# A long-convolution kernel whose first stage loads 50 rows out of 64 in small strided pieces instead of whole blocks of 128 partitions

## The chip, the core and the metric

The kernel runs on one NeuronCore of a Trainium2 chip. The metric is device time in microseconds (us) for one launch, lower is better. Matmuls run on TensorE (PE in the profile; its weight loads are PEld), elementwise work on VectorE (DVE), ScalarE (ACT) and GpSimd (POOL). Transfers between HBM and the on-chip memory SBUF (128 partitions) are issued from three instruction queues: SyncE (SP), ACT and POOL. All of them are carried out by the same 16 DMA engines.

## The reference

The inputs are x and v of shape (4, 12800, 128), a table of positions of shape (12800, 64), and small weights. With S = 12800:

```python
h = (np.maximum(pos_emb @ w1, 0.0) @ w2) * np.exp(-0.01 * np.arange(S))[:, None]
y = irfft(rfft(x * v, n=2 * S, axis=1) * rfft(h, n=2 * S, axis=0), n=2 * S, axis=1)[:, :S]
z = x * y                                   # the long convolution, gated by x
gate = sigmoid(sum(conv_w[k] * shift(z, 4 - k) for k in range(5)))
out = (gate * (z @ w_val)) @ w_out
```

## The kernel before, in words

The long transform is cut in two: position n of the sequence is split into a slow index n1 (two halves j of N1 = 100) and a fast index n2 of N2 = 64. The work goes through three stages.

The **first stage** transforms x * v along n1, one n2 at a time (function spectra), and between these steps it computes the transform of the filter h out of the position table (generator filt). For each n2 the rows n1 and 99 - n1 are folded, so 50 rows (NF) are left for each pair of batches. The host lays them out as two halves of 64 rows (NH), 50 rows of data and 14 rows of zeros, one half on partitions 0 to 63 and the other on 64 to 127. In this input (xv) one n2 is 128 rows of 2048 numbers: x and v side by side.

The steps of one n2 are these. **fetch** (L311) loads one block of 128 x 2048 from xv to one of five buffers called ld, on SP. **product** (L317, DVE) multiplies the x half by the v half; for every second n2 the result goes to a tile u, for the others back to ld. **mirrored** (L325 and L326, DVE) takes two n2, q and 63 - q, and forms sum and difference, the tiles eo. **spectra** (L338, PE) multiplies them by the table fold, and ACT copies the result from PSUM to a tile st (L340), of which there are four. **store** (L345) writes st to a_u in HBM: 96 of its 100 rows from ACT's queue, the last 4 from POOL's. A pair of n2 thus costs two fetches, two stores, and 24 matmuls of 512 columns.

The order is written out by hand: at step n of 64 the program issues fetch(n + 7), product(n + 3), every second time mirrored, then spectra(n), as many steps of filt as a budget gives, and the store. The first 16 steps of filt (L257) read the position table, which comes in 16 loads of 128 x 400 numbers (function load_pos, L250, SP), each issued when a place in a sixth ld buffer is free. Later steps of filt are L275 to L277 (result in ag) and L286 to L300.

The **second stage** (50 steps p) loads a pair of spectra from a_u (L232) and its weights (L226) into the same six ld buffers, multiplies with the filter and transforms back along n2, and stores to c_y. From its step 34 on it also loads parts of c_y to ag for the third stage, 64 rows at first, then 16 and 80 (load_k, L207). The **third stage** transforms back along n1, gates, and does the short convolution and the two projections.

Completion of DMAs: the program hands out eight counters (DMAHW0 to DMAHW7 below) in turn to the DMAs of SP and ACT together. A DMA that gets a counter still in use waits on its queue until the DMA that had it before has landed. POOL's DMAs have eight of their own (DMASW).

Of the kernel before, what the change touches and what calls it, by code (L numbers as in the profile page):

```python
# [9 lines left out]
F32 = mybir.dt.float32  # L10
# [3 lines left out]
ALU = mybir.AluOpType  # L14
# [9 lines left out]
B, S, D, FO, KC = 4, 12800, 128, 64, 5  # L24
J, N1, N2 = 2, 100, 64
M = N1 * N2
KG = 8
NF, NH = N1 // 2, 64
R = 4
WARM = 2  # L30
NC1 = N1 // 2 + 1
# [3 lines left out]
def _tables():  # L35
# [7 lines left out]
    for r in (0, NH):  # L43
        fold[r:r + NF, 0, :N1] = np.cos(off) + np.sin(off)
        fold[r:r + NF, 1, :N1] = np.cos(off) - np.sin(off)
# [84 lines left out]
def tile_longconv_gate(  # L130
# [56 lines left out]
    def load():  # L187
        return ld.tile([128, 2048], F32, name="ld")
# [3 lines left out]
    ld_pool = tc.tile_pool(name="ld", bufs=6)  # L192
    ld = ld_pool.__enter__()
# [28 lines left out]
    def load_pair(p, n1=None):  # L222
        if p % PG == 0:
            n_p = min(PG, NP - p)
            wt = load().rearrange("p (k c e) -> p k c e", k=PG, c=4)[:, :, 0:3]
            nc.sync.dma_start(out=wt[:, 0:n_p], in_=t_w[:, p:p + n_p])  # L226
            weights.append(wt)
        a2 = load().rearrange("p (k j e) -> p k j e", k=2, j=J)
        if n1:
            load_a(a2, p, 0, n1)  # L230
        else:
            nc.sync.dma_start(  # L232
                out=a2.rearrange("p k j e -> p k (j e)"),
                in_=a_u[2 * p:2 * p + 2].rearrange("k s n e j b d -> (s n e) k (j b d)"))
        return a2, weights[-1][:, p % PG]

    with tc.tile_pool(name="p1", bufs=1) as p1, tc.tile_pool(name="ps1", bufs=1, space=PSUM) as ps1:
        g_sb = p1.tile([N1, J, FO, N2], F32, name="g_sb")

        GN, E, XB = 8, 4, 5  # L240
        held = [load() for _ in range(XB + 1)]
        PE1 = GN // 2 * N1
        pos_held = held.pop()[:, 0:2048 // PE1 * PE1].rearrange("p (i q a) -> p i q a", q=GN // 2, a=N1)
        parts, pos_ts = [(c0, j) for c0 in range(0, N2, GN) for j in range(J)], []

        def load_pos():
            if len(pos_ts) < len(parts):
                c0, j = parts[len(pos_ts)]
                t = pos_held[:, len(pos_ts) % (2048 // PE1)]
                nc.sync.dma_start(out=t.rearrange("p q a -> p (q a)"), in_=pos[j, c0 // GN])  # L250
                pos_ts.append(t)

        def filt():
            for i, (n0, j) in enumerate(parts):
                gp = ps1.tile([N1, GN, FO], F32, name="gp", bufs=2)
                for q in range(GN // 2):
                    nc.tensor.matmul(  # L257
                        out=gp[:, 2 * q:2 * q + 2].rearrange("a n e -> a (n e)"),
                        lhsT=pos_ts[i][:, q], rhs=w1bd, start=True, stop=True)
                nc.vector.scalar_tensor_tensor(  # L260
                    g_sb[:, j, :, n0:n0 + GN], gp.rearrange("a n e -> a e n"), 0.0,
                    win[:, j, n0:n0 + GN].unsqueeze(1).to_broadcast([N1, FO, GN]),
                    op0=ALU.max, op1=ALU.mult)
                load_pos()
                yield 1.5
# [41 lines left out]
        n_seq = [n for q in range(N2 // 2) for n in (q, N2 - 1 - q)]  # L307

        def fetch(i):
            t = held[i % XB]  # L310
            nc.sync.dma_start(out=t, in_=xv[n_seq[i]].rearrange("h q w j l b d -> (h q) (w j l b d)"))  # L311
            fetched[i] = t.rearrange("p (w e) -> p w e", w=2)

        def product(i):
            t = fetched.pop(i)
            u = p1.tile([128, J * 2 * XE], F32, name="u", bufs=1) if i % 2 == 0 else t[:, 0]
            nc.vector.tensor_tensor(u, t[:, 0], t[:, 1], op=ALU.mult)  # L317
            us[i] = u

        def mirrored(q):  # L320

            a, b = us.pop(2 * q), us.pop(2 * q + 1)
            eo = held_e[q % 2]
            for s, op in ((0, ALU.add), (1, ALU.subtract)):
                nc.vector.tensor_tensor(eo[:, s].rearrange("p j l e -> p (j l e)"), a, b, op=op)  # L325
                nc.vector.tensor_tensor(eo[:, s, :, 0], eo[:, s, :, 0], eo[:, s, :, 1], op=ALU.subtract)  # L326
            eos[q] = eo
# [22 lines left out]
        with tc.manual_schedule():  # L350
            held_e = [p1.tile([128, 2, J, 2, XE], F32, name=f"eo{i}") for i in range(2)]
            fetch(0)
            raws = [
# [5 lines left out]
            for i in range(1, XB):  # L359
                fetch(i)  # L360
                load_pos()
            product(0)
            product(1)
            mirrored(0)
            product(2)
            for i in (XB, XB + 1):
                fetch(i)
            for n in range(N2):
                q, s = divmod(n, 2)
                if n + XB + 2 < N2:  # L370
                    fetch(n + XB + 2)
                if n + 3 < N2:
                    product(n + 3)
                if s == 0 and q + 1 < N2 // 2:
                    mirrored(q + 1)
                st = spectra(q, s)
# [20 lines left out]
    with tc.tile_pool(name="p2", bufs=1) as p2, tc.tile_pool(name="psz", bufs=1, space=PSUM) as psz, \  # L397
# [62 lines left out]
        with tc.manual_schedule():  # L460
            for p in range(-1, NP + 1):
# [53 lines left out]
                if nxt:  # L515
                    spectrum(p + 1, 1)
                if old:
# [7 lines left out]
                    inverse(p - 1, 1, ((0, oa[:, 2]), (1, oa[:, 3, 0:PB]), (0, oc[:, 0]), (1, oc[:, 1])))  # L525

# [250 lines left out]
```

## Time and profile before

| what | us |
|---|---|
| median of three runs (lowest, highest) | 1134.86 (1127.76, 1135.0) |
| the profiled execution, its own time | 1130.9 |
| its span, first to last instruction | 1128.9 |
| start of the second stage's first matmul | 341.2 |

The profiled execution lies 4 us below the median, and 2 us of its time lie outside the span. Over the whole span PE is busy 92%, DVE 87%, POOL 62%, ACT 55%, and the DMA engines move 317 GB/s on average. These are means over three stages with different limits. The first stage is the first 341 us, so the views below are cut to it. In the lists of waits, "A <- B" says that A stood idle until B released it. SPq, ACTq and POOLq are the instruction queues that issue DMAs.

### The profile page before, as it was taken

The page shows a single profiled execution, that of the slowest core. Times are in us where ns is not written, and L with a number is a line of the kernel's source. Part 1 is how long each engine was busy: PE and PEld are TensorE (multiplying, and loading weights), DVE is VectorE, ACT ScalarE, POOL GpSimd, SP SyncE. Part 2 cuts the span into 40 slices and gives each one's busy share as a digit, 9 for nine tenths or more (in the row PEclk, how much of TensorE's full clock was granted, in tenths as well). Part 3 has the DMA queues.
Part 4 walks back from the last instruction along what each step waited for, and adds up shares of the span by engine and source line. Part 5 has one row for each costly group of instructions (what it writes and reads, how often), then busy time and mean ns, then how long its engine had stood idle before and what let it go on. Part 6 is the DMA issues. An engine that isn't in the chain of part 4 may idle for free.

```text
span 1128.9 us, 17155 instructions
## 1 busy us (share of the span) xinstructions
PE 1038.0 (92%) x6204; PEld 490.9 (43%) x6204; DVE 980.8 (87%) x1214; ACT 619.1 (55%) x1003; POOL 698.1 (62%) x405
## 2 busy tenths in 40 slices
PE   5789997977868999999999999979999999999996
PEld 2345654534423444444444444434444444444442
DVE  6677657888817999999999999739999999999997
ACT  1347665866642444444344444346767777767673
POOL 1111110100016888898898889638999899999981
PEclk9899999999986999999999999998999999999999
DMA  9999999999987788888988999566888888888842
GB/s 376 414 415 410 395 380 368 391 371 372 338 263 245 257 302 310 304 298 309 315 302 288 373 339 329 163 193 262 342 318 346 305 349 314 350 313 351 314 181 116
DMA packets 87771, 357.95 MB, mean 317 GB/s; under 512 B 9269, under 2 KB 18278, under 8 KB 65073
## 3 DMA queue, kind: packets, MB, share of 16 engines
q1 hardware_dynamic: 45768, 224.74, 55.0%
q10 hardware_dynamic: 39408, 129.18, 29.3%
q0 software_dynamic: 2512, 2.94, 0.9%
q8 instruction: 50, 0.82, 0.3%
q14 instruction: 33, 0.26, 0.1%
HBM read 225.76 MB, written 131.07 MB: 316 GB/s over the span
## 4 chain that ended last, share of the span: by engine, by line
PE 63%; DMA 22%; DVE 11%; ACT 3%; issue 1%; SPq 0%; ACTq 0%; DVEq 0%
PE c_ps L442 20%; DMA ld<-in_xv_dram 17%; PE sd L601 9%; PE z_ps L426 9%; PE o_ps L664 7%; PE v_ps L654 6%; PE tp L615 5%; PE fp L338 3%; DMA ld<-in_pos_dram 3%; PE c_ps L411 2%; DVE gt L643 2%; DVE eo L325 2%; DMA c_y<-c_sb 1%; DVE va L432 1%; DVE vb L432 1%
## 5 line engine op out<-in xcount | busy, mean ns | idle before, releaser
L628 POOL TENSOR_TENSOR ext<-yr,xr 128x400 f32<-128x400 f32 x120 | 304.4, 2538 | 38.1 <-DVE yr L626 32.7
L643 DVE SCALAR_TENSOR_TENSOR gt<-ext,cw,gt 128x1600 f32<-128x1600 f32 x128 | 242.7, 1896 | 2.4 <-ACT gt L640 2.4
L338 PE MATMUL fp<-eo,fold 64*128 64x512 f32 x768 | 194.8, 643 | 35.2 <-ACT st L340 19.0
L446 ACT COPY c_sb<-c_ps 128x1024 f32<-128x1024 f32 x100 | 101.3, 1013 | 207.3 <-PE c_ps L442 207.3
L345 POOL DMA_DIRECT2D a_u<-st x64 | 33.2, 519 | 290.4 <-ACT st L340 245.2
L340 ACT COPY st<-fp 128x1024 f32<-128x1024 f32 x128 | 126.7, 1016 | 117.9 <-PE fp L338 81.7
L442 PE MATMUL c_ps<-va,ld 64*128 64x512 f32 (+1 forms) x800 | 165.7, 554 | 0.0
L432 DVE TENSOR_TENSOR va<-z_ps,h_sb 128x2048 f32<-128x2048 f32 x50 | 114.5, 2290 | 30.4 <-PE z_ps L426 30.4
L426 PE MATMUL z_ps<-ld 64*64 64x512 f32 x800 | 123.0, 619 | 9.8 <-DMA ld<-a_u 8.7
L601 PE MATMUL sd<-ag,fold 100*64 100x512 f32 (+1 forms) x512 | 127.9, 617 | 2.9 <-DMA ag<-c_y 2.9
L509 POOL TENSOR_TENSOR va<-va,vb 128x1024 f32<-128x1024 f32 x49 | 116.0, 2367 | 15.9 <-DVE vb L432 15.9
L338 PEld LDWEIGHTS fp<-eo,fold 64*128 64x128 f32 x768 | 73.4, 199 | 115.4 <-issue 59.8
L442 PEld LDWEIGHTS c_ps<-va,ld 64*128 64x128 f32 x800 | 74.1, 189 | 112.2 <-issue 111.7
L664 PE MATMUL o_ps<-gd,wout 128*128 128x400 f32 x256 | 111.5, 517 | 10.7 <-DVE gd L659 9.8
L513 POOL TENSOR_TENSOR va<-va,vb 128x1024 f32<-128x1024 f32 x50 | 119.1, 2383 | 0.0
L432 DVE TENSOR_TENSOR vb<-z_ps,h_sb 128x2048 f32<-128x2048 f32 x50 | 114.0, 2281 | 0.0
L608 ACT COPY sd_sb<-sd 128x512 f32<-128x512 f32 x128 | 76.7, 599 | 57.6 <-PE sd L601 57.0
L654 PE MATMUL v_ps<-ext,wval 128*128 128x400 f32 x256 | 107.3, 501 | 0.0
L442 PE MATMUL c_ps<-vc,ld 64*128 64x512 f32 x400 | 94.2, 589 | 0.0
L615 PEld LDWEIGHTS tp<-ident,sd_sb 128*128 128x128 f32 x512 | 58.9, 142 | 79.2 <-PE sd L601 48.7
L510 POOL TENSOR_TENSOR vc<-vc,vd 128x768 f32<-128x768 f32 x49 | 89.2, 1820 | 1.9
L615 PE MATMUL tp<-ident,sd_sb 128*128 128x128 f32 x512 | 81.0, 283 | 4.7 <-ACT sd_sb L608 3.4
(86 smaller groups left out, 1484.9 us busy)
## 6 DMA issues: line engine op xcount, KB each, us to landing
ld<-in_xv_dram SPq DMA_DIRECT2D x64, 1024.0 KB
ag<-c_y SPq DMA_DIRECT2D x58, 1024.0 KB
c_y<-c_sb ACTq DMA_DIRECT2D x100, 512.0 KB
a_u<-st ACTq DMA_DIRECT2D x64, 768.0 KB
ld<-a_u SPq DMA_DIRECT2D x48, 1024.0 KB
xr<-in_xt_dram SPq DMA_DIRECT2D x31, 800.0 KB
out_dram<-o_sb ACTq DMA_DIRECT2D x31, 800.0 KB
ld<-in_tab_w_dram SPq DMA_DIRECT2D x12, 768.0 KB
```

Of the source, the lines that this page charges most:

```text
L338: nc.tensor.matmul(out=fp[:, h], lhsT=fold[r, w], rhs=eo[r, o, :, l], start=i == 0, stop=i == len(terms) - 1)
L340: nc.scalar.copy(out=st[:, o].rearrange("k j (h b) d -> k h j (b d)", h=2), in_=fp)
L426: nc.tensor.matmul(out=zs[c][half[h]], lhsT=wk[half[c], 0, half[h]], rhs=a2[half[c], h, j], start=True, stop=True)
L432: nc.vector.tensor_tensor(out, z.rearrange("p (b d) -> p b d", d=D).unsqueeze(1).to_broadcast([128, n, B, D]), h_sb.unsqueeze(2).to_broadc ...
L442: nc.tensor.matmul(out=c_ps[:, h, 0:n], lhsT=wk[half[h], 1 + c], rhs=vt[half[h]].rearrange("p b d -> p (b d)"), start=(i == 0), stop=(i == ...
L513: nc.gpsimd.tensor_tensor(va[:, 2:4], va[:, 2:4], vb[:, 2:4], op=ALU.add)
L601: nc.tensor.matmul(out=sd[c * N2:(c + 1) * N2], lhsT=inv[k, s // NG, c], rhs=ct[c][k, r * B * D:(r + 1) * B * D], start=True, stop=True)
L615: nc.tensor.transpose(out=tp[:, b], in_=t[:, b], identity=ident)
L628: nc.gpsimd.tensor_tensor(e[:, r0 + r], yr, xr, op=ALU.mult)
L643: nc.vector.scalar_tensor_tensor(gt, rows(t, k), cw[:, k:k + 1], gt, op0=ALU.mult, op1=ALU.add)
L654: nc.tensor.matmul(out=v_ps, lhsT=wval, rhs=rows(t)[:, r * ROW:(r + 1) * ROW], start=True, stop=True)
L664: nc.tensor.matmul(out=o_ps, lhsT=wout, rhs=gd, start=True, stop=True)
```

## The change

A pair of n2 now has one load step. The host puts the 50 rows of a half on 64 partitions in a new pattern (QROW): rows 0 to 47 on the partitions whose number modulo 8 is 0 to 5, six in each group of eight; rows 48 and 49 on partitions 6 and 38 of the half. The table fold is permuted in the same way, so PE's work is the same. The zeros are not loaded any more: two of the three buffers for a pair are set to zero once by DVE and POOL, and the loads leave those partitions alone. The third buffer gets its zeros with pair 0, which is loaded whole.

fetch(q) is now six DMAs on SP, each of 16 rows (partitions r, r + 8, ..., r + 120) of 4096 numbers, 16 KB a row and 256 KB a DMA, and one DMA on POOL of 4 rows (partitions 6, 38, 70, 102). For pair 0 it is eight DMAs on SP. There are three buffers of two blocks where five blocks were before. product writes both n2 of a pair to u. The position table is loaded in four DMAs of 128 x 1600 into the space of ag, which is written only after the table has been read. The six ld buffers become one tile, and the second stage takes its places from a list (spare), in the order in which they come free.

```diff
+KX = 6
+QROW = np.array([8 * (q // 6) + q % 6 if q < 48 else 6 + 32 * (q - 48) for q in range(NF)])
...
     for r in (0, NH):
-        fold[r:r + NF, 0, :N1] = np.cos(off) + np.sin(off)
-        fold[r:r + NF, 1, :N1] = np.cos(off) - np.sin(off)
+        fold[r + QROW, 0, :N1] = np.cos(off) + np.sin(off)
+        fold[r + QROW, 1, :N1] = np.cos(off) - np.sin(off)
...
     def load():
-        return ld.tile([128, 2048], F32, name="ld")
+        return ld[:, spare.pop(0)]
...
-    ld_pool = tc.tile_pool(name="ld", bufs=6)
-    ld = ld_pool.__enter__()
+    ld_pool = tc.tile_pool(name="ld", bufs=1)
+    ld = ld_pool.__enter__().tile([128, 6, 2048], F32, name="ld")
+    spare, used = [4, 5, 0, 1, 2, 3], {}
...
+            used["w", p // PG] = spare[0]
+        used["a", p] = spare[0]
...
-        GN, E, XB = 8, 4, 5
-        held = [load() for _ in range(XB + 1)]
+        GN, E, XB = 8, 4, 3
         PE1 = GN // 2 * N1
-        pos_held = held.pop()[:, 0:2048 // PE1 * PE1].rearrange("p (i q a) -> p i q a", q=GN // 2, a=N1)
-        parts, pos_ts = [(c0, j) for c0 in range(0, N2, GN) for j in range(J)], []
-
-        def load_pos():
-            if len(pos_ts) < len(parts):
-                c0, j = parts[len(pos_ts)]
-                t = pos_held[:, len(pos_ts) % (2048 // PE1)]
-                nc.sync.dma_start(out=t.rearrange("p q a -> p (q a)"), in_=pos[j, c0 // GN])
-                pos_ts.append(t)
+        parts = [(c0, j) for c0 in range(0, N2, GN) for j in range(J)]
+
+        pos_ts = ag.rearrange("p k j e -> p (k j e)")[:, 0:len(parts) * PE1].rearrange(
+            "p (i q a) -> p i q a", q=GN // 2, a=N1)
+
+        def load_pos(i):
+            nc.sync.dma_start(out=pos_ts[:, 4 * i:4 * i + 4].rearrange("p i q a -> p (i q a)"), in_=pos[i])
...
-                        lhsT=pos_ts[i][:, q], rhs=w1bd, start=True, stop=True)
+                        lhsT=pos_ts[:, i, q], rhs=w1bd, start=True, stop=True)
...
-                load_pos()
...
-        n_seq = [n for q in range(N2 // 2) for n in (q, N2 - 1 - q)]
-
-        def fetch(i):
-            t = held[i % XB]
-            nc.sync.dma_start(out=t, in_=xv[n_seq[i]].rearrange("h q w j l b d -> (h q) (w j l b d)"))
-            fetched[i] = t.rearrange("p (w e) -> p w e", w=2)
-
-        def product(i):
-            t = fetched.pop(i)
-            u = p1.tile([128, J * 2 * XE], F32, name="u", bufs=1) if i % 2 == 0 else t[:, 0]
-            nc.vector.tensor_tensor(u, t[:, 0], t[:, 1], op=ALU.mult)
-            us[i] = u
+        def fetch(q):
+            t = ld[:, 2 * (q % XB):2 * (q % XB) + 2].rearrange("p e n -> p (e n)")
+            for r in range(KX if q else 8):
+                nc.sync.dma_start(out=t[r:128:8], in_=xv[q, r])
+            if q:
+                nc.gpsimd.dma_start(out=t[KX:128:32], in_=xv[q, KX, 0:16:4])
+            fetched[q] = t.rearrange("p (e w n) -> p e w n", e=2, w=2)
+
+        def product(q):
+            t = fetched.pop(q)
+            us[q] = p1.tile([128, 2, J * 2 * XE], F32, name="u", bufs=1)
+            for e in range(2):
+                nc.vector.tensor_tensor(us[q][:, e], t[:, e, 0], t[:, e, 1], op=ALU.mult)
...
-            a, b = us.pop(2 * q), us.pop(2 * q + 1)
+            u = us.pop(q)
             eo = held_e[q % 2]
             for s, op in ((0, ALU.add), (1, ALU.subtract)):
-                nc.vector.tensor_tensor(eo[:, s].rearrange("p j l e -> p (j l e)"), a, b, op=op)
+                nc.vector.tensor_tensor(eo[:, s].rearrange("p j l e -> p (j l e)"), u[:, 0], u[:, 1], op=op)
...
+            for q in range(1, XB):
+                (nc.vector, nc.gpsimd)[q - 1].memset(ld[:, 2 * q:2 * q + 2], 0.0)
             fetch(0)
+            load_pos(0)
...
-            for i in range(1, XB):
-                fetch(i)
-                load_pos()
             product(0)
+            mirrored(0)
+            for q in range(1, XB):
+                fetch(q)
+                load_pos(q)
+            load_pos(XB)
             product(1)
-            mirrored(0)
-            product(2)
-            for i in (XB, XB + 1):
-                fetch(i)
+            fetch(XB)
+            fetch(XB + 1)
             for n in range(N2):
                 q, s = divmod(n, 2)
-                if n + XB + 2 < N2:
-                    fetch(n + XB + 2)
-                if n + 3 < N2:
-                    product(n + 3)
                 if s == 0 and q + 1 < N2 // 2:
                     mirrored(q + 1)
+                if s == 1 and q + 2 < N2 // 2:
+                    product(q + 2)
+                    if q + 2 + XB < N2 // 2:
+                        fetch(q + 2 + XB)
                 st = spectra(q, s)
...
+                    spare.append(used.pop(("a", p + 1)))
...
+                    if p % PG == 0:
+                        spare.append(used.pop(("w", p // PG - 1)))
...
-    xv = np.concatenate([xv, np.zeros_like(xv[:, :, :NH - NF])], 2)
+    xz = np.zeros(xv.shape[:2] + (NH,) + xv.shape[3:], xv.dtype)
+    xz[:, :, QROW] = xv
+    xz = np.stack([xz[:N2 // 2], xz[:N2 // 2 - 1:-1]], 1).reshape(N2 // 2, 2, 16, 8, -1)
+    xv = np.transpose(xz, (0, 3, 2, 1, 4)).reshape(N2 // 2, 8, 16, -1)
     pos = np.asarray(inputs["pos_emb"]).reshape(J, N1, N2 // KG, KG // 2, 2, FO)
-    pos = np.transpose(pos, (0, 2, 4, 5, 3, 1)).reshape(J, N2 // KG, 2 * FO, KG // 2 * N1)
+    pos = np.transpose(pos, (2, 0, 4, 5, 3, 1)).reshape(4, 4, 2 * FO, KG // 2 * N1)
+    pos = np.transpose(pos, (0, 2, 1, 3)).reshape(4, 2 * FO, 2 * KG * N1)
```

On SP, which carries the loads, these are the first issues before and after (ld<-in_xv_dram is a load of x and v, in_pos_dram the position table):

```order
L311 DMA ld<-in_xv_dram 128x2048 x2
L250 DMA ld<-in_pos_dram 128x400
L311 DMA ld<-in_xv_dram 128x2048
L250 DMA ld<-in_pos_dram 128x400
L311 DMA ld<-in_xv_dram 128x2048
L250 DMA ld<-in_pos_dram 128x400
```

```order
L312 DMA ld<-in_xv_dram 16x4096 x8
L254 DMA ag<-in_pos_dram 128x1600
L312 DMA ld<-in_xv_dram 16x4096 x6
L254 DMA ag<-in_pos_dram 128x1600
L312 DMA ld<-in_xv_dram 16x4096 x6
L254 DMA ag<-in_pos_dram 128x1600 x2
L312 DMA ld<-in_xv_dram 16x4096 x174
```

The position table moved to the front, four issues where 16 were spread over the first 16 steps, and 64 loads of x and v became 194. In the middle of the stage, again on SP, with what each issue waits for (DVE is the product that frees the buffer), before and after:

```order
L311 DMA ld<-in_xv_dram 128x2048 [waits DMAHW4_49,DVE_49]
L311 DMA ld<-in_xv_dram 128x2048 [waits DMAHW6_49,DVE_49]
L311 DMA ld<-in_xv_dram 128x2048 [waits DMAHW0_49,DVE_49]
L311 DMA ld<-in_xv_dram 128x2048 [waits DMAHW2_49,DVE_49]
L311 DMA ld<-in_xv_dram 128x2048 [waits DMAHW4_49,DVE_49]
```

```order
L312 DMA ld<-in_xv_dram 16x4096 [waits DMAHW6_49,DVE_49]
L312 DMA ld<-in_xv_dram 16x4096 [waits DMAHW7_49]
L312 DMA ld<-in_xv_dram 16x4096 [waits DMAHW0_49]
L312 DMA ld<-in_xv_dram 16x4096 [waits DMAHW1_49]
L312 DMA ld<-in_xv_dram 16x4096 [waits DMAHW2_49]
L312 DMA ld<-in_xv_dram 16x4096 [waits DMAHW4_49]
L312 DMA ld<-in_xv_dram 16x4096 [waits DMAHW6_49,DVE_49]
```

Before, a load used the counter of the load four earlier (4, 6, 0, 2, then 4 again), now that of the load six earlier, which is the same piece of the pair before. The six pieces of one pair and its two stores take up all eight counters. On POOL, the first stores of the last 4 rows (a_u<-st) and what stands ahead of them, before and after:

```order
L182 DMA win<-in_tab_win_dram 100x128
L180 DMA w1bd<-in_w_dram 64x64 x2
L345 DMA a_u<-st 4x2048 x2
L388 DMA fwd<-in_tab_fwd_dram 100x300
L345 DMA a_u<-st 4x2048
```

```order
L185 DMA win<-in_tab_win_dram 100x128
L356 MEMSET ld 128x4096
L183 DMA w1bd<-in_w_dram 64x64 x2
L314 DMA ld<-in_xv_dram 4x4096 x4
L348 DMA a_u<-st 4x2048
L314 DMA ld<-in_xv_dram 4x4096
L348 DMA a_u<-st 4x2048
L394 DMA fwd<-in_tab_fwd_dram 100x300
```

POOL's queue now holds a load that waits for a product on DVE ahead of every second store. PE's and ACT's instructions are the same and in the same order in all three stages.

## The prediction

> **What bounds the kernel now.** I read the profile in this order: the rows in 40 slices, the chain that ended last (cut to the first 345 us), the DMA queues, then the waits. Of the slices:
>
> ```profile
> DMA  9999999999987788888988999566888888888842
> GB/s 376 414 415 410 395 380 368 391 371 372 338 263 245 257 302 310 304 298 309 315 302 288 373 339 329 163 193 262 342 318 346 305 349 314 350 313 351 314 181 116
> ```
>
> One slice is 28.2 us. In the first eleven the DMA engines are busy nine tenths or more and move 338 to 415 GB/s. The edit is in these slices. Their chain:
>
> ```profile
> by line: DMA ld<-in_xv_dram 54.4%; PE fp L338 9.7%; DMA ld<-in_pos_dram 8.7%; DVE eo L325 5.5%; ACT st L340 2.9%; DVE ld L317 2.8%; DVE eo L326 2.6%; DVE u L317 2.3%; DMA a_u<-st 1.9%; DVE fk L289 1.9%; issue 1.3%; PE gp L257 0.9%; DMA ld<-
> ...
> 1.19 7.95 DMA ld<-in_xv_dram
> ...
> 15.78 13.44 DMA ld<-in_pos_dram
> ...
> 29.70 16.68 DMA ld<-in_pos_dram
> ...
> 341.17 2.11 PE z_ps L426 x8
> ```
>
> 63% of the chain is loads. The first two loads of 1 MB needed 7.95 us together; a position load of 0.2 MB that takes 16.68 stands in line behind others. The second stage begins at 341.17. So the first stage ends when its bytes are through, and each edit is worth what it does to the time of the 16 DMA engines. How full these are, and what each queue gets out of them, in the 232 us between start and end (first the windows, with PE, PEld, DVE, ACT, POOL, clock, DMA share and GB/s; then the queues, q1 from SP, q10 from ACT, q0 from POOL):
>
> ```profile
> 64.00:296.00 232.00, 204.99 (x1550) 114.76 (x1552) 176.44 (x276) 156.42 (x244) 26.17 (x50) 0.97 0.99 385
> ```
>
> ```profile
> q1 hardware_dynamic: 6965, 49.60, 56.0%
> q10 hardware_dynamic: 5357, 37.63, 40.5%
> q0 software_dynamic: 1617, 1.75, 2.6%
> ```
>
> A share of 0.99 leaves no slack. A queue's MB over its share of the window is its rate had it all 16 engines: SP's loads 49.60 / (0.560 x 232 us) = 382 GB/s, ACT's stores 37.63 / (0.405 x 232) = 400, POOL's pieces 1.75 / (0.026 x 232) = 290.
>
> **The change, part by part.** The sizes:
>
> ```profile
> ld<-in_xv_dram SPq DMA_DIRECT2D x64, 1024.0 KB
> a_u<-st ACTq DMA_DIRECT2D x64, 768.0 KB
> ```
>
> ```profile
> ld<-in_pos_dram SPq DMA_DIRECT2D x16, 200.0 KB
> a_u<-st POOLq DMA_DIRECT2D x64, 32.0 KB, 6.7
> ```
>
> *Removed.* A pair of n2 loads 2 x 1024 KB = 2.097 MB, which is 2.097 / 0.382 = 5.49 us of all engines. After the change it is 6 x 256 KB = 1.573 MB on SP and 64 KB = 0.066 MB on POOL, the latter 0.066 / 0.290 = 0.23 us. Were SP's rate to stay, a pair would cost 1.573 / 0.382 + 0.23 = 4.35 us, 1.14 us less, and the 31 pairs behind pair 0 35 us less. This is the good end.
>
> *The rate of the new pieces.* The trace has no DMA of 16 rows eight partitions apart. It has loads of fewer than 128 rows: those of L207, 64 neighbouring rows in the second stage. Four are issued there, the first and the last here:
>
> ```profile
> 605.39 0.52 SPq L207 DMA_DIRECT2D ag<-c_y  x1
> ...
> 635.70 0.47 SPq L207 DMA_DIRECT2D ag<-c_y  x1
> ```
>
> The stretches in which these four were carried, and their q1:
>
> ```profile
> 606.70:609.90 3.20, 3.20 (x26) 1.46 (x26) 3.20 (x5) 1.14 (x2) 2.61 (x3) 1.00 1.00 214
> 616.00:619.80 3.80, 3.80 (x38) 1.31 (x34) 3.80 (x6) 2.07 (x4) 3.49 (x3) 1.00 1.02 302
> 632.10:635.80 3.70, 3.70 (x38) 1.54 (x38) 3.70 (x3) 2.15 (x4) 3.65 (x2) 1.00 1.01 276
> 641.80:648.40 6.60, 6.60 (x52) 2.88 (x48) 6.60 (x7) 2.79 (x5) 5.73 (x4) 1.00 1.04 353
> ```
>
> ```profile
> q1 hardware_dynamic: 120, 0.68, 99.7%
> ...
> q1 hardware_dynamic: 167, 0.82, 69.3%
> ...
> q1 hardware_dynamic: 132, 0.67, 72.1%
> ...
> q1 hardware_dynamic: 295, 1.34, 58.7%
> ```
>
> The engines count as fully busy and yet move 214 to 353 GB/s. In each, 0.524 MB are the 64-row load; the rest of q1 are loads over 128 partitions, which I take out at 382 GB/s. What is left: 0.524 / (3.19 - 0.41) = 188 GB/s, 0.524 / (2.63 - 0.77) = 282, 0.524 / (2.67 - 0.38) = 229, 0.524 / (3.87 - 2.14) = 301. These loads filled 87%, 49%, 62% and 26% of the engines' time: the more of it they fill, the slower they are, as if they blocked each other but not the stores. Six loads of 16 neighbouring rows (L207 too) come lower still, in the 7.0 us from 725.4 on:
>
> ```profile
> q1 hardware_dynamic: 190, 0.77, 64.7%
> ```
>
> 0.77 / (0.647 x 7.0) = 170 GB/s. So rows few in number and close together are slow. The new pieces are as few as these but spread as wide as a full load, so the 64-row load lies between the two ends, and I take it. In the changed stage stores keep about 40% of the engines as in q10's row, loads the rest, which lies between the 49% and 62% cases: the middle of 282 and 229, 256 GB/s. A pair then costs 1.573 / 0.256 + 0.23 = 6.37 us, 0.88 more than now, 27.3 us over 31 pairs. The other ends: 282 gives +10, 229 gives +50, 188 (no stores beside) +96.
>
> [...]
>
> *Pair 0* is loaded in eight pieces, 2.097 MB, and no store runs beside them: at 188 GB/s 11.2 us in place of 5.5, +5.7 us before PE can start.
>
> *Positions.* PE no longer stands still for the 13.4 and 16.7 us of the two position loads in the chain. But the engines carry these 3.28 MB as before, at full share, so the stall goes to the next load of x and v: 0. If DMA were not full it would be worth up to those 30 us.
>
> *SP's issues.* Two per pair become six:
>
> ```profile
> 40.37 0.33 SPq L311 DMA_DIRECT2D ld<-in_xv_dram  x1
> ```
>
> ```profile
> SPq L311 <- DMA ld<-in_xv_dram: 162.1, 40, 8.1
> ```
>
> 6 x 0.33 = 2.0 us; a pair takes nearly 10 (5.49 of loads and, at 400 GB/s, 2 x 0.786 / 0.400 = 3.9 of stores): hidden. The second row shows SP standing until an earlier load lands, its counter being taken. Four loads (4.2 MB) could be under way, now six pieces (1.6 MB). A load lands 7.95 - 5.49 = 2.5 us later than its bytes alone need; with 0.33 us for the issue a piece's place is empty for 2.8 us, while the five others keep the engines for 5 x 0.262 / 0.256 = 5.1 us: hidden. If they land together, the cover is gone and a pair costs 2.8 us more.
>
> *Waits on POOL and ACT.* POOL's piece waits for DVE's product, and every second 4-row store stands behind it. Its store takes 6.7 us to land, and the tile st is wanted again only four n2, some 20 us, later: 0. ACT's store now waits for the store two n2 back, about 10 us old, and ACT's copies stand behind it; a store's 0.79 MB take 2.0 us, 3.9 when loads take turns with them, and 2.5 to land: 0, with PE waiting for st if not.
>
> ```profile
> 1.01 0.27 DVE L176 MEMSET w2bd<- 128x256 f32 x1
> ```
>
> ```profile
> L509 POOL TENSOR_TENSOR va<-va,vb 128x1024 f32<-128x1024 f32 x49 | 116.0, 2367 | 15.9 <-DVE vb L432 15.9
> ```
>
> *The two memsets* of 4096 a partition: DVE 16 x 0.27 = 4.3 us, POOL between that and 4 x 2.37 = 9.5. Pair 0 needs longer, and pair 2, which waits for POOL, stands behind pair 1: 0. Products are the same 64. The second stage's new list of places lets loads start no later: 0.
>
> *Sum*: 27.3 + 5.7 = +33 us; span 1128.9 + 33 = 1161.9, and with the 2 us outside it **1164 us**, 2.6% above the median of the runs.
>
> **The rivals.**
>
> *The loads keep their rate* (faster). For it: the rows reach over all 128 partitions, and stores take turns with them at nearly 1 to 1, so two loads seldom need to meet. Against: the stretch at 49%, with stores beside, still gave 282. The end is -35 us; but PE sets a part of the stage:
>
> ```profile
> 113.00:170.00 57.00, 56.06 (x626) 33.88 (x624) 36.25 (x55) 37.42 (x40) 6.33 (x13) 1.00 1.00 388
> ```
>
> In these 57 us, some six pairs, PE has no gap, so 6 x 1.14 = 7 us can't be had: 1131 - 28 = **1103**. It decides from about 330 GB/s on: 1.573 / 0.330 + 0.23 = 5.00, -0.49 x 31 = -15, +5.7 for pair 0.
>
> *It cancels*: at 301 GB/s a pair costs 5.23 + 0.23 = 5.46, the same as now, and pair 0 leaves +5: **1136**. For it: the stretch with most else beside. Against: loads there filled only 26%.
>
> *Bytes are not removed at all*: the rows of zeros would have to be free now. Against it the 1024 KB of each load. No chance of its own.
>
> *Slower still*: six pieces land together and the queue runs empty, 2.8 us a pair on top (33 + 87 = +120), or the rate is 188 all through (+96 + 5.7 = +102): **1233 to 1251**. Against: stores fill such gaps.
>
> **How the numbers follow.** My forecast, 229 to 282 GB/s, with 1147 to 1187 us: 0.50. Slower still: 0.12. Cancels: 0.18. Rate kept: 0.20. The range leaves out the best of the faster cases and the worst of the slower: 1104 to 1195. About 1% is what measurement can tell from no change. Slower by more than 1% means over 1146, which from 1131 takes a rate under 282, so it has the forecast and the still slower case: 0.62. Within 1%: 0.18. Faster: 0.20.
>
> **What would show it.** In the changed profile the page's read bytes fall by some 13 MB; the first twelve slices still show nine tenths of DMA but under 360 GB/s; SP's queue moves its MB at 230 to 280 GB/s of full share where it had 382; the second stage's first matmul comes near 374 us instead of 341; position loads are gone from the chain; the stages behind are unchanged. A first stage under 330 us, or a rate of q1 over 330 GB/s, would prove me wrong; a DMA share well under 0.95 there would mean that a queue runs dry, not that rows are slow.

## The result and the profile after

| | before | after |
|---|---|---|
| median (runs of the comparison) | 1132.88 us (4) | 1164.89 us (4; 1163.16 to 1167.13) |
| ratio after / before, 95% interval | | 1.0315 [1.0282, 1.0348] |
| span of the profiled execution | 1128.9 us | 1161.4 us |
| start of the second stage's first matmul | 341.17 us | 374.86 us |

The change is 3.1% slower, 32 us, and the whole loss lies in the first stage. From the second stage's first matmul to the end, before needs 1128.9 - 341.2 = 787.7 us and after 1161.4 - 374.9 = 786.5. That matmul in after's timeline (start, length in us, in brackets the idle time ahead and what ended it):

```profile
374.86 3.80 PE L432 MATMUL z_ps<-ld 64*64 64x512 f32 x16 [7.39 <-DMA ld<-a_u]
```

The slices and the bytes on the page of after (a slice is now 29.0 us):

```profile
DMA  9999999999998688888888998685888888888842
GB/s 208 241 328 320 313 305 309 327 310 326 318 344 273 255 291 304 302 290 307 293 302 303 338 375 306 228 212 210 337 332 318 351 301 347 323 340 328 328 186 113
...
HBM read 211.53 MB, written 131.07 MB: 295 GB/s over the span
```

The same last row on the page of before:

```profile
HBM read 225.76 MB, written 131.07 MB: 316 GB/s over the span
```

14.2 MB less are read, just what the diff takes out (31 pairs x 0.459 MB). The first twelve digits of the DMA row are still 9: the engines count as full all the time, and carry less. The windows of after say how much less (columns as in the prediction):

```profile
0.00:28.00 28.00, 9.40 (x38) 4.72 (x40) 10.01 (x9) 3.31 (x3) 7.19 (x11) 1.00 0.95 204
28.00:56.00 28.00, 6.03 (x20) 3.21 (x18) 13.91 (x15) 1.93 (x2) 2.80 (x5) 0.61 1.02 234
64.00:296.00 232.00, 201.00 (x1520) 109.59 (x1518) 163.13 (x240) 135.80 (x196) 40.26 (x73) 0.95 0.98 319
```

and the start of before in the same windows:

```profile
0.00:28.00 28.00, 15.44 (x68) 7.99 (x68) 18.83 (x22) 5.33 (x5) 3.71 (x10) 1.00 0.95 375
28.00:56.00 28.00, 20.52 (x100) 10.87 (x102) 18.54 (x22) 9.83 (x10) 5.36 (x10) 0.88 1.02 414
```

The DMA share (last but one) is the same in both kernels. The rate is about half over the first 56 us, and 319 against 385 GB/s after that. So there are two losses, and the windows size both:

- *Steady.* A pair was 2.097 MB of loads and 1.573 MB of stores, at 385 GB/s 9.53 us. Now it is 1.639 + 1.573 = 3.212 MB, at 319 GB/s 10.07 us: +0.54 us, over 31 pairs +17 us.
- *Start.* In 56 us the engines moved 28 x (0.204 + 0.234) = 12.3 MB. At the steady 319 GB/s it would have been 17.9, so 5.6 MB are late: 5.6 / 0.319 = 17.5 us. In before the same 56 us moved 22.1 MB, about what its steady rate of 385 GB/s gives (21.6).

Together some 34 us. The queues of after in the steady window tell which transfers are slow:

```profile
q1 hardware_dynamic: 4205, 34.37, 48.7%
q10 hardware_dynamic: 5096, 35.84, 43.2%
q0 software_dynamic: 2441, 3.53, 5.8%
```

Per full share: SP's loads 34.37 / (0.487 x 232) = 304 GB/s (382 before), ACT's stores 35.84 / (0.432 x 232) = 358 (400), POOL's pieces 3.53 / (0.058 x 232) = 262 (290). The stores were not touched by the change and are slower all the same. The chain of after, cut to 380 us:

```profile
by line: DMA a_u<-st 46.2%; DMA ld<-in_xv_dram 24.9%; PE fp L341 10.2%; DMA ld<-in_tab_w_dram 4.2%; ACT st L343 4.0%; PE ap L277 2.9%; issue 1.4%; SPq L312 1.1%; DVE u L321 0.7%; DMA ld<-a_u 0.6%; DVE va L438 0.6%; DVE vb L438 0.6%; ACTq L3
...
47.34 10.72 DMA ld<-in_xv_dram
...
68.53 11.03 DMA a_u<-st
```

Loads up to 58 us, then mostly stores (46.2%), with the position loads gone. DMA holds three quarters of it, where the lines of before's chain that the prediction shows add up to two thirds. Why a store ends the chain is in the waits of ACT (total us, times, longest):

```profile
ACT st L343 <- DMA ld<-in_xv_dram: 43.1, 5, 26.6
ACT st L343 <- DMA a_u<-st: 41.9, 16, 4.5
```

ACT's copies stand behind its stores, and its stores behind their counters. The one wait of 26.6 us is for the first store, whose counter belongs to a load of pair 3, issued at 36.9 us and landed at 51.3 (the expectation of experiment 3 calls it a load of pair 4). Its group in the timeline, after and then before:

```profile
L348 ACTq DMA_DIRECT2D a_u<-st x64: 310/310/354, 51.3 to 366.3; - x64
```

```profile
L345 ACTq DMA_DIRECT2D a_u<-st x64: 310/311/358, 19.0 to 331.3; - x64
```

The first store is 32 us late, the last one 35. It is tempting to call this wait the cause. The third experiment shows that it is not the main one.

### The profile page after: what moved, and what is told of

It reads as the page before. It is cut to its first block, busy times and chain, and to the rows that moved or that the text cites. A ratio compares the mean times of both kernels' runs of the same rounds, so it can differ in the third digit from the quotient of the medians.

```text
span 1161.4 us, 17425 instructions
## 1 busy us (share of the span) xinstructions
PE 1042.3 (90%) x6204; PEld 488.6 (42%) x6204; DVE 983.4 (85%) x1215; ACT 616.5 (53%) x1003; POOL 721.1 (62%) x437
## 4 chain that ended last, share of the span: by engine, by line
PE 64%; DMA 26%; DVE 5%; ACT 4%; issue 1%; SPq 0%; ACTq 0%; DVEq 0%
PE c_ps L448 20%; DMA a_u<-st 15%; PE sd L610 10%; PE z_ps L432 9%; DMA ld<-in_xv_dram 8%; PE o_ps L673 7%; PE v_ps L663 6%; PE tp L624 5%; PE fp L341 3%; PE c_ps L417 2%; DMA ld<-in_tab_w_dram 1%; DVE gt L652 1%; ACT st L343 1%; DVE va L438 1%; PE ap L277 1%
## 5 line engine op out<-in xcount | busy, mean ns | idle before, releaser
L341 PE MATMUL fp<-eo,fold 64*128 64x512 f32 x768 | 200.9, 660 | 76.9 <-ACT st L343 58.3
L328 DVE TENSOR_TENSOR eo<-u 128x1024 f32<-128x1024 f32 x64 | 78.0, 1219 | 33.2 <-PE fp L341 32.9
L321 DVE TENSOR_TENSOR u<-ld 128x1024 f32<-128x1024 f32 x64 | 75.4, 1219 | 19.4 <-DMA ld<-in_xv_dram 18.8
```

The lines of the kernel that those rows point to most:

```text
L341: nc.tensor.matmul(out=fp[:, h], lhsT=fold[r, w], rhs=eo[r, o, :, l], start=i == 0, stop=i == len(terms) - 1)
```

## The experiments

The theories, as the expectations name them. **A**: what is slow is where a piece's 16 rows lie; the author's guess is that rows 32 partitions apart get in each other's way, and a piece with rows 8 apart is full of them. **B**: a DMA of few rows is slow wherever they lie. **C**: it is the regrouping (pairs in one buffer of 2 blocks, positions first, three buffers) and not the pieces. **D**: it is the start, where the first stores wait for the counters of pairs 3 and 4. **E**: it is the row's length, 16 KB in place of 8. **G**: it is the shared counters: eight DMAs a pair use all of them, so that stores and loads wait for each other.

All intervals are 95% and of the ratio to before, measured beside it. The code cuts show the lines that matter; those of experiments 10 to 12 are against experiment 6, the others against the change.

**1. Rows 7 apart** (A against B). The six pieces of a pair lie on partitions 8 + r, 15 + r, ... instead of r, r + 8, ...; the fold table is permuted to match.

```diff
-                nc.sync.dma_start(out=t[r:128:8], in_=xv[q, r])
+                nc.sync.dma_start(out=t[8 + r:8 + r + 106:7] if q else t[r:128:8], in_=xv[q, r])
...
-                nc.gpsimd.dma_start(out=t[KX:128:32], in_=xv[q, KX, 0:16:4])
+                nc.gpsimd.dma_start(out=t[21:106:28], in_=xv[q, KX, 0:16:4])
```

> The six pieces of a pair take rows 7 partitions apart (from partition 8 + r) in place of 8, so that of the 16 rows of a piece hardly two lie 32 partitions apart; number, size and order of the DMAs, the memsets and pair 0 stay. The 4 rows of POOL move to partitions 21, 49, 77, 105. Theory A (rows 32 partitions apart block each other): a 16 KB row alone falls from 1.23 us towards 0.62 to 0.8, SP's rate between 64 and 296 us rises from 304 to over 360 GB/s, ACT's stores from 358 to over 385, the first store leaves before 40 us in place of 51, time 1105 to 1135. Theory B (small pieces, few rows, few DMAs under way are slow as such): nothing moves, 1165 within 4.

Measured: 1157.21 us (1149.95 to 1158.63), ratio 1.0204 [1.0151, 1.0256]. Between the two. The queues of this kernel in the steady window:

```profile
q10 hardware_dynamic: 5341, 37.51, 46.4%
q1 hardware_dynamic: 4208, 34.46, 43.7%
```

SP's loads went from 304 to 34.46 / (0.437 x 232) = 340 GB/s with nothing changed but the place of the rows: so the place matters. But the stores, at 37.51 / (0.464 x 232) = 348, did not rise with them, and most of the loss stayed. Neither theory had this.

**2. One whole load per pair** (C). The new program as it is, but each pair comes in one DMA of 128 rows of 16 KB, zeros and all.

```diff
-            for r in range(KX if q else 8):
-                nc.sync.dma_start(out=t[r:128:8], in_=xv[q, r])
-            if q:
-                nc.gpsimd.dma_start(out=t[KX:128:32], in_=xv[q, KX, 0:16:4])
+            nc.sync.dma_start(out=t, in_=xv[q])
```

> Each pair is loaded whole, zeros too, by one DMA of 128 rows of 16 KB; pairs, positions in ag, order and memsets stay, POOL's piece goes. Theories A and B: SP's rate is back at 380 GB/s, stores at 400, time 1120 to 1140. Rival C (the loss comes from loading in pairs, from the prologue's order or from the list of places): it stays over 1155 although 14 MB more are moved at the old rate.

Measured: 1126.92 us, ratio 0.9963 [0.9941, 0.9986]. Its windows:

```profile
0.00:28.00 28.00, 14.49 (x68) 7.61 (x68) 21.66 (x22) 7.10 (x7) 7.17 (x11) 1.00 0.95 380
64.00:296.00 232.00, 203.26 (x1528) 110.69 (x1526) 172.88 (x274) 150.80 (x239) 24.86 (x47) 0.96 0.98 388
```

The rates of before are back, 380 and 388 GB/s, with rows of 16 KB. C falls: all that the change does beside the pieces is worth 4 us in its favour. The pieces cost the 32 us and these 4, though they load 22% less.

**3. Pairs 3 and 4 fetched later** (D). The two fetches stand behind the first two stores, so that these get free counters.

```diff
-            fetch(XB)
-            fetch(XB + 1)
...
+                if n < 2:
+                    fetch(XB + n)
```

> The fetches of pairs 3 and 4 move from the prologue to behind the first and second store in program order, so that the first stores on ACT don't get counters that those loads hold. Theory D (the start is lost because ACT's first store waits 26 us for a load of pair 4, so that loads run without stores beside them): the first store leaves at 25 to 35 us in place of 51, GB/s in the first 56 us rise from 219 to over 270, time 1140 to 1155. Theory A alone: the same bytes at the same mutual blocking, 1160 to 1168.

Measured: 1160.19 us (1159.97 to 1163.7), ratio 1.0259 [1.0222, 1.0295]. The group of stores in its timeline:

```profile
L348 ACTq DMA_DIRECT2D a_u<-st x64: 310/311/342, 38.5 to 364.8; - x64
```

The first store came 13 us sooner (38.5 against 51.3), the last only 1.5, and the intervals of the two ratios overlap. The first 56 us moved 216 and 258 GB/s in the two windows, 237 on average, short of the 270 that D asked for, and the steady window 315. D falls as the main cause.

**4. Rows of 8 KB** (E). Each row of a piece is read from two places of 8 KB.

```diff
+            t2 = t.rearrange("p (e n) -> p e n", e=2)
...
-                nc.sync.dma_start(out=t[r:128:8], in_=xv[q, r])
+                nc.sync.dma_start(out=t2[r:128:8], in_=xv[q, r].rearrange("e i n -> i e n"))
```

> Each 16 KB row is read from two places of HBM, 8 KB each, so that it should travel as two packets of 8 KB; all else stays. Theory E (rows of 16 KB take two of three turns at an engine and starve the stores, whose packets are 8 KB): ACT's stores go from 358 GB/s to over 380, time 1150 to 1160. Theory A: a row costs twice 0.62 us alone, stores as before, 1165 within 5.

Measured: 1154.43 us (1149.97 to 1161.11), ratio 1.0205 [1.0152, 1.0259]. Its steady window and the queues in it:

```profile
64.00:296.00 232.00, 208.37 (x1570) 113.43 (x1569) 178.37 (x266) 144.76 (x215) 44.07 (x78) 0.96 1.01 335
```

```profile
q1 hardware_dynamic: 6567, 35.88, 49.7%
q10 hardware_dynamic: 5386, 37.83, 44.5%
```

335 GB/s where the change has 319; the loads at 35.88 / (0.497 x 232) = 311, the stores at 366. A part of the loss, some 10 us, goes away with shorter rows. The time lies in E's range, but the stores stay under the 380 that E asked for, the loads themselves are hardly faster, and the second experiment has 16 KB rows at full speed. E is a side effect at most.

**5. A ruler.** Ahead of the kernel's own work, test loads of 16 rows of 16 KB on SP, first one at a time, then streams of six without waits between.

```diff
+            for start, step, n in ((0, 8, 16), (11, 7, 16), (8, 7, 16), (0, 1, 16), (0, 4, 8)):
+                for j in range(4):
+                    piece(1, j, start, step, n)
+                pause()
+            for starts, step in (((0,) * 6, 8), (tuple(range(6)), 8), ((11,) * 6, 7), (tuple(range(8, 14)), 7)):
+                for j, start in enumerate(starts):
+                    piece(j, j, start, step)
+                pause()
```

piece(i, j, start, step, n) loads n rows into buffer i, to the partitions start, start + step and so on; pause() issues nine tiny loads that set the groups apart.

> The changed kernel with test loads ahead of its first stage (SP only, nothing else on the DMA engines, results overwritten later). One at a time, four each, 16 KB rows: 16 rows 8 apart; 16 rows 7 apart from 11; 16 rows 7 apart from 8; 16 neighbours; 8 rows 4 apart. Then six without a wait between them: 8 apart from 0; 8 apart from 0 to 5; 7 apart from 11; 7 apart from 8 to 13. [...] Theory B (16 rows are slow as such): 1.0 to 1.23 for each, whatever the step. Its time as a whole says nothing.

Windows within the four streams of its one run: 8 apart, all on the same partitions; 8 apart from 0, 1, ... 5; 7 apart on the same partitions; 7 apart from 8, 9, ... 13:

```profile
137.00:143.00 6.00, 0.00 (x0) 0.00 (x0) 0.00 (x0) 0.00 (x0) 0.00 (x0) 1.00 0.94 190
161.00:166.00 5.00, 0.00 (x0) 0.00 (x0) 0.00 (x0) 0.00 (x0) 0.00 (x0) 1.00 0.99 210
185.00:189.00 4.00, 0.00 (x0) 0.00 (x0) 0.00 (x0) 0.00 (x0) 0.00 (x0) 1.00 0.78 262
207.00:211.00 4.00, 0.00 (x0) 0.00 (x0) 1.60 (x1) 0.00 (x0) 1.41 (x1) 1.00 0.85 262
```

A row's mean time on its engine is 16 engines x 16.4 KB x share / rate, that is 0.262 MB x share / rate (with 200 GB/s as 0.200 MB/us): 8 apart 1.30 and 1.24 us, 7 apart 0.78 and 0.85. So pieces 8 apart, by themselves and with nothing else running, move 190 to 210 GB/s, about what the change's start shows (204 and 234). Single loads, one at a time, hardly told the spacings apart: four of them were issued within 10.9 us with rows 8 apart, within 9.2 and 10.0 us with rows 7 apart, and within 12.6 us as 16 neighbours.

**6. Pieces of 32 rows, 4 apart.** Three pieces of 512 KB instead of six of 256 KB; 48 rows on the partitions with numbers 0 to 2 modulo 4, the last two of a half on 3 and 35. Same bytes as the change, but three loads and two stores a pair on the eight shared counters where the change has six and two. A in its first form has to call them as slow, since they too hold partitions 32 apart.

```diff
-KX = 6
+KX = 3
...
-QROW = np.array([8 * (q // 6) + q % 6 if q < 48 else 6 + 32 * (q - 48) for q in range(NF)])
+QROW = np.array([4 * (q // 3) + q % 3 if q < 48 else 3 + 32 * (q - 48) for q in range(NF)])
...
-                nc.sync.dma_start(out=t[r:128:8], in_=xv[q, r])
+                nc.sync.dma_start(out=t[r:128:4], in_=xv[q, r])
...
-                nc.gpsimd.dma_start(out=t[KX:128:32], in_=xv[q, KX, 0:16:4])
+                nc.gpsimd.dma_start(out=t[KX:128:32], in_=xv[q, KX, 0:32:8])
```

> [...] Theory A: 1160 to 1168. Theory G (the counters: only two stores and six small loads under way): 1140 to 1152, and ACT's waits for a store before fall under 20 us.

Measured: **1107.07 us** (1104.13 to 1110.92), ratio **0.9794 [0.9758, 0.9829]**. Faster than both kernels, and missed by both expectations. Its windows and, in the steady one, its queues:

```profile
0.00:28.00 28.00, 10.39 (x48) 5.47 (x48) 18.49 (x19) 3.35 (x4) 8.30 (x13) 1.00 0.94 321
28.00:56.00 28.00, 26.03 (x126) 13.80 (x128) 22.74 (x26) 11.62 (x12) 8.37 (x15) 0.88 1.01 397
64.00:296.00 232.00, 214.68 (x1612) 117.09 (x1612) 188.17 (x296) 164.81 (x260) 42.22 (x76) 0.99 0.98 360
```

```profile
q10 hardware_dynamic: 5822, 40.83, 47.0%
q1 hardware_dynamic: 4212, 38.95, 45.9%
```

Loads at 38.95 / (0.459 x 232) = 366 GB/s, stores at 374, the start at 321 and 397. The change's idea, fewer bytes, does pay when the pieces have this shape.

**7. The start alone.** The change, with pairs 0 to 4 loaded whole (from an input of their own), the others in pieces.

```diff
+            if q < 5:
+                nc.sync.dma_start(out=t, in_=xw[q])
+            for r in range(KX if q >= 5 else 0):
...
-            if q:
+            if q >= 5:
```

> Pairs 0 to 4 are loaded whole by one DMA of 128 rows, pairs 5 to 31 in pieces as before. It splits the loss between the start, where loads run alone, and the rest. If the start costs what the traces say (eighth store 29 us later than before the change, of which some 20 us remain at the end), 1140 to 1148; if the prediction's split were right (5.7 us for the start, 27 us for the pieces further on), 1156 to 1162.

Measured: 1145.26 us, ratio 1.0123 [1.0088, 1.0157]. 20 us of the loss are the start, as its expectation said for that case; the windows above gave 17.5.

**8. Without POOL's 4-row loads.** Rows 48 and 49 are left out of pairs 1 to 31.

```diff
-            if q:
-                nc.gpsimd.dma_start(out=t[KX:128:32], in_=xv[q, KX, 0:16:4])
```

> POOL's load of 4 rows is left out of pairs 1 to 31, so rows 48 and 49 of each half are missing in what is computed. If these loads cost only their share of the engines (0.23 to 0.3 us a pair), 1155 to 1159; if POOL's wait for the product holds up stores, under 1150; if they are hidden, 1164 within 3.

Measured: 1151.78 us, ratio 1.0196 [1.0157, 1.0234], between the cases of its expectation: 13 us less than the change (give or take some 6, an estimate from the two intervals), where their bytes at POOL's rate are 31 x 0.23 = 7. The start of this kernel:

```profile
0.00:28.00 28.00, 9.27 (x40) 4.72 (x40) 13.98 (x13) 3.31 (x3) 6.06 (x9) 1.00 0.96 232
28.00:56.00 28.00, 8.80 (x36) 4.25 (x36) 12.91 (x15) 3.85 (x4) 1.13 (x3) 0.70 1.01 262
```

In 56 us the engines move 13.8 MB where the change moves 12.3: 1.6 MB, or 5 us at 319 GB/s. In the steady window 320 GB/s carry 3.146 MB a pair, 9.83 us against 10.07, which is 7 us over 31 pairs. So about 5 of the 13 us lie at the start; why 4-row loads weigh more there was not tested.

**9. The second ruler** (the cause). Theory A needed a form that has 16 rows 8 apart slow and 32 rows 4 apart fast. **A'** keeps the place of the rows as the cause and names the places: 32 rows 4 apart and 64 rows 2 apart, on every fourth and every second of the 128 partitions, should be as fast as whole loads; 32 rows 2 apart and 64 neighbours, which stay within one half, as slow as 16 rows 8 apart. Why a place should be slow, it leaves open. The rival **B'** is the mere number of rows. Streams of six as before, of 16 KB rows:

```diff
+            for n, step, starts in ((32, 4, (0,) * 6), (32, 4, (0, 1, 2, 3, 0, 1)), (32, 2, (0,) * 6), (64, 2, (0,) * 6),
+                                    (64, 1, (0,) * 6), (96, 1, (0,) * 6), (16, 8, (0,) * 6), (128, 1, (0,) * 6)):
+                for j, start in enumerate(starts):
+                    nc.sync.dma_start(
+                        out=places[j][start:start + step * (n - 1) + 1:step],
+                        in_=xv[8 + j].rearrange("r i e -> (r i) e")[0:n])
+                pause()
```

> Before the change's own work, streams of six 16 KB-row loads are issued on SP without waits: 32 rows 4 apart from partition 0; 32 rows 4 apart from 0, 1, 2, 3, 0, 1; 32 rows 2 apart; 64 rows 2 apart; 64 neighbours; 96 neighbours; 16 rows 8 apart; 128 rows. [...] If only the number of rows in a DMA decides (rival B'), everything of 32 rows and more takes 0.61 to 0.70 and only the 16 rows are slow. The time of the whole kernel is the change's plus the streams', some 100 us, and says nothing else.

Windows within the streams, in this order: 32 rows 4 apart (from several partitions, not shown, they move 380); 32 rows 2 apart; 64 rows 2 apart; 64 neighbours; 96 neighbours; 16 rows 8 apart; 128 rows:

```profile
4.00:11.00 7.00, 0.00 (x0) 0.00 (x0) 0.00 (x0) 0.00 (x0) 0.00 (x0) 1.00 0.98 382
...
54.00:67.00 13.00, 0.00 (x0) 0.00 (x0) 0.00 (x0) 0.00 (x0) 0.00 (x0) 1.00 1.03 211
86.00:99.00 13.00, 0.00 (x0) 0.00 (x0) 0.00 (x0) 0.00 (x0) 0.00 (x0) 1.00 1.00 426
118.00:146.00 28.00, 0.00 (x0) 0.00 (x0) 0.00 (x0) 0.00 (x0) 0.00 (x0) 1.00 1.02 209
166.00:204.00 38.00, 0.00 (x0) 0.00 (x0) 0.00 (x0) 0.00 (x0) 0.00 (x0) 1.00 1.00 230
222.50:228.00 5.50, 0.00 (x0) 0.00 (x0) 0.00 (x0) 0.00 (x0) 0.00 (x0) 1.00 1.15 232
250.00:276.00 26.00, 0.00 (x0) 0.00 (x0) 3.47 (x1) 0.00 (x0) 4.62 (x3) 1.00 1.01 398
```

The third and the fourth row shown are the experiment: both are 64 rows of 16 KB, 1 MB a load. Every second partition of 128 goes at 426 GB/s, the lower 64 partitions at 209: 0.615 us a row against 1.28. And 32 rows are fast 4 apart (382 GB/s) and slow 2 apart (211). So B' falls. All four come out as A' says, and so do the 16 rows 8 apart (0.262 x 1.15 / 0.232 = 1.30 us a row; the window is short). Nor does only the half count, partitions 0 to 63 or 64 to 127: 16 rows 8 apart lie in both and are slow. The engines show as full in the slow cases too (shares of 1.02 and 1.03, beside 1.00 and 0.98 in the fast ones): a slow row is simply longer on its engine. Which engine carries which row is not in the trace, so why a place is slow, and whether the 32 partitions of theory A have to do with it, is not shown; the rates by layout are measured.

Two more things stay open. 96 neighbours move 230 GB/s, hardly more than the 64 at 209, though they reach into both halves. And experiment 1, whose rows lie 7 apart as in the faster streams of the first ruler (262 GB/s at shares of 0.78 and 0.85), still moved only 255 GB/s from 28 to 56 us, at a share of 0.98.

**10 and 11. Counters** (G). Experiment 6 gains 58 us on the change, and it also has fewer DMAs, five a pair on the shared counters and not eight. The tenth kernel adds three loads of one row of 64 bytes, so that there are eight again. The eleventh moves the last 4 rows from POOL's queue to SP's, which makes six.

```diff
+                if q:
+                    nc.sync.dma_start(out=t[7 + 4 * r:8 + 4 * r, 0:16], in_=xv[q, KX, 1 + r:2 + r, 0:16])
```

```diff
-                nc.gpsimd.dma_start(out=t[KX:128:32], in_=xv[q, KX, 0:32:8])
+                nc.sync.dma_start(out=t[KX:128:32], in_=xv[q, KX, 0:32:8])
```

> The version with 32 rows a load (1107.1 us) has five DMAs a pair on the eight shared counters where the change has eight. This one adds three loads of one row of 64 bytes of zeros a pair on SP, so that a pair uses eight counters as in the change, and moves no more data worth counting. If the 32-row pieces gain through the rows' speed (theory A'), it stays at 1105 to 1115. If a good part of the gain is that fewer counters make fewer waits (theory G), it goes to 1130 or more.

> The version with 32 rows a load (1107.1 us), with the four last rows of a pair loaded on SP's queue instead of POOL's. In the change these loads cost 13 us (by leaving them out), where their share of the DMA engines' time made 7. If the rest is the way by POOL (its wait for the buffer and its own queue), this one is 3 to 8 us faster, 1099 to 1104; if the rows cost the same wherever they come from, 1105 to 1110; if SP's queue of issues is what is short, more than 1110.

Measured: 1122.6 us, ratio 0.9929 [0.9899, 0.996], and 1124.04 us, ratio 0.9942 [0.991, 0.9974]. Both came out some 16 us above experiment 6, the tenth between its two theories, the eleventh in its worst case. With eight DMAs a pair, 32-row pieces still beat the change by 3.9% (the difference of the two ratios, in parts of before): that is the shape of the pieces, the place of their rows and their size together, which only the rulers tell apart. The other 1.4% went with three DMAs that carry next to nothing. Where it goes is not settled. ACT's waits for DMAs, which G would lengthen, are 26.5 + 19.6 us in the tenth and 35.1 + 10.2 in the sixth. First the tenth:

```profile
ACT st L345 <- DMA a_u<-st: 26.5, 11, 4.5
...
ACT st L345 <- DMA ld<-in_xv_dram: 19.6, 2, 13.7
```

```profile
ACT st L343 <- DMA a_u<-st: 35.1, 20, 4.8
...
ACT st L343 <- DMA ld<-in_xv_dram: 10.2, 3, 6.0
```

Their sums are alike, 46.1 and 45.3 us; in the eleventh these waits are 8.2 + 45.0. SP's queue has time to spare in the eleventh, where it stands waiting for a product on DVE that frees its buffer:

```profile
SPq L312 <- DVE u L321: 55.1, 10, 8.6
```

That does not name the cause either: experiment 12 below has 68.7 us of the same wait and loses nothing. What the steady windows do show is a lower rate than the 360 GB/s of the sixth, in the tenth and then in the eleventh:

```profile
64.00:296.00 232.00, 207.62 (x1572) 113.64 (x1574) 180.70 (x280) 156.83 (x247) 41.50 (x75) 0.97 0.96 345
64.00:296.00 232.00, 207.04 (x1558) 113.99 (x1558) 176.78 (x278) 155.81 (x244) 25.86 (x50) 0.96 0.95 339
```

**12. Two of the three pieces in one.** 64 rows 2 apart and 32 rows 4 apart, the same partitions as experiment 6, four DMAs a pair.

```diff
+            nc.sync.dma_start(out=t[0:128:2], in_=xv[q, 0:64])
+            nc.sync.dma_start(out=t[1:128:4], in_=xv[q, 64:96])
```

> The same 50 rows on the same partitions as in the version with 32 rows a load (1107.1 us), but two of its three 32-row pieces are one load of 64 rows, 2 apart, so that a pair has four DMAs on the shared counters and not five. Three DMAs more a pair cost 15.5 us (1122.6), so one less should give some 5 if the waits for counters go on shrinking (theory G): 1099 to 1104, 0.975 of before or less. If five are already few enough, 1105 to 1109. More than 1110 if a load of 1 MB lands too late for the next pair.

Measured: 1110.92 us (1105.47 to 1111.76), ratio 0.9821 [0.9778, 0.9864], not to be told from experiment 6 (0.9794). Another DMA less brings nothing more, so the count of DMAs is not a cost that simply adds up.

## Why the prediction was right

The forecast of 1164 us met 1164.89, with the right bound and the right direction. That the two agree to 1 us is luck: two terms of its sum were off by some 10 us each in opposite directions, and the steady loss came mostly by a way that the sum had at nothing.

- *The bound, DMA engines that count as full.* Right. Share 0.98 in the steady window, the first twelve slices at nine tenths, 14.2 MB less read (some 13 were forecast), the second stage at 374.86 us (near 374). Its mark against a queue that runs dry, a share under 0.95, didn't show.
- *The rate of the new pieces, 256 GB/s in the steady stage, +27.3 us.* The direction was right and the size wrong: SP's loads run at 304 GB/s there, outside the 230 to 280 it named and short of the 330 that would have refuted it. It chose 256 for a share of the loads between 49% and 62%; the loads held 48.7%. At 304 a pair's load costs 1.573 / 0.304 + 0.066 / 0.262 = 5.43 us, as much as the 5.49 before. By itself this term would be nothing.
- *"As if they blocked each other but not the stores."* This step failed. The stores fell from 400 to 358 GB/s: 1.573 / 0.358 - 1.573 / 0.400 = +0.46 us a pair, 14 us over 31 pairs. That is nearly the whole steady loss of 17 us, and the sum had 0 there. Why the stores slow down was not shown: in experiment 1 faster loads left them at 348, in experiment 4 they rose to 366 beside loads that stayed slow.
- *Pair 0, +5.7 us.* Mis-sized, 17.5 us by the windows and 20 by experiment 7. The rate was about right (188 without stores beside; the start shows 204), but it was applied to pair 0 alone. The program issues five pairs before the first store, so no stores run beside the other four either. They were priced at 256.
- *POOL's pieces, 0.23 us a pair.* About right in the steady window, too small at the start: without them the kernel is 13 us faster, not 7, and some 5 of the 13 lie in the first 56 us (experiment 8).
- *Costed at nothing.* Regrouping, memsets and the new list of places: right, experiment 2 puts them and the positions together at -4 us. SP's issues: not told apart from the rates; in experiment 10 three tiny loads more a pair cost 15 us, so the number of DMAs may have a price. ACT's wait for counters: it does come, 43.1 and 41.9 us, but that it costs time is not shown. Experiment 2 is as fast as before with 64.8 us of waits for stores, and the wait at the start, 26.6 us long, mattered little when it was shortened (experiment 3).
- *The rivals.* "The loads keep their rate" had a fair price, 1103 us: experiment 6 comes near that case, 1107, with pieces of another shape and loads at 366 GB/s, not 382. "Slower still" did not occur.

## What to carry to other kernels

A DMA's share of busy time says nothing of its speed (64 rows went at 426 GB/s with a share of 1.00 and at 209 with 1.02): divide the bytes of a queue by its share of the engines and compare that rate with a load of all 128 partitions. To leave out rows of a load (rows of 16 KB here), keep every piece spread over the 128 partitions with 32 rows or more (every 4th or every 2nd partition, 382 and 426 GB/s alone in experiment 9), not 16 rows 8 apart (190 to 232) and not a block of neighbours (209 for 64, 230 for 96); with fewer DMAs a pair as well, that made 1107 us here against 1165 for the same bytes. Price the start of a stage apart from its middle, since transfers that later take turns with others run alone there (204 and 234 GB/s in the change's first 56 us, 319 in its steady window).

## What the runs showed that was not expected

- 64 rows on every second partition load at 426 GB/s, 64 neighbouring rows at 209, with the engines shown as full in both (experiment 9). 96 neighbours reach 230, hardly more than 64.
- Loads in pieces came with slower stores: ACT's stores of 96 rows went at 400 GB/s beside whole loads (before, experiment 2), at 358 beside the change's 16-row pieces and 348 beside those of experiment 1, at 374 beside 32-row pieces.
- Three loads of 64 bytes a pair, on SP's queue, cost 15 us in all (experiment 10), and moving four rows a pair from POOL's queue to SP's cost 17 (experiment 11). The rate of the engines falls, from 360 GB/s to 345 and 339, but no view names the wait.
